# Three column counts instead of five for the matmuls of a mixture's first product

## The chip, the core and the metric

The kernel runs on one core of a Trainium2 chip. The metric is the time of one execution on the device, in microseconds (us).

## What is computed

The reference is causal attention with a decay, followed by a mixture of experts that sends every token to one expert:

```python
scores = np.where(causal, -1e9, scale * q @ k.T + decay)      # 8 batches, 8 heads, 576 tokens, 64
attn_out = softmax(scores) @ v                                # -> x: 4608 tokens x 512
expert_idx = np.argmax(x @ w_gate, axis=1)                    # 8 experts
for e in range(8):
    mask = expert_idx == e
    h = np.maximum(x[mask] @ w1[e], 0.0)                      # w1: 512 x 1024
    out[mask] = gate_w[mask, None] * (h @ w2[e])              # w2: 1024 x 512
```

How many tokens an expert gets is known only on the chip. With the inputs timed here the counts are 582, 620, 632, 571, 592, 462, 604 and 545 for experts 0 to 7.

## The kernel before

The first half of the program is attention, and nothing of it is touched. Then the experts come one after the other. Each has room for 640 tokens (`CAP`). An expert's work on TensorE (PE) is the *first product* (tokens times `w1`, line 1421, function `product`) followed by the *second product* (ReLU'd values `h` times `w2`, line 1229, function `down`). Every value is split into a rounded high part and a low rest, and a product is three matmuls: high by high, low by high, high by low.

Expert 0 has a path of its own. For experts 1 to 7 the first product is done by a scheme with seven block products in place of eight, on pairs of tokens: token columns are halved to `HN` = 320 and the tokens' and weights' blocks are combined by sums first. The work is in four rounds (`seven`, i = 0 to 3). A round has seven *steps* of 6 matmuls, in two groups: steps 0 to 3 (24 matmuls) and steps 4 to 6 (18 matmuls). The program order of every engine is pinned to the order in which the code is written. Between the groups' steps the other engines do the rest of a round:

- ACT copies the product of step 0 to `p1` (line 1475) and of step 2 to `p5` (line 1481), and makes ReLUs (`hhw`, line 1466);
- VectorE (DVE) adds `p1` (lines 1478 and 1486), combines (1487, 1494) and makes the low parts of `h` (line 1469);
- GpSimd (POOL) makes one sum, `p5` = `u3` + `p5` (line 1488), from the DVE result of line 1486, and ACT's ReLU of it comes before ACT's copy of the next round's step 0 in ACT's order;
- in the same queues stand tasks for other stages: splits of weights into high and low part (ACT lines 1333 and 1348, DVE and POOL lines 1339 and 1349), sums of the next expert's weights (POOL 1318 to 1321) and gathers of its tokens (POOL 1149).

PE's second group of a round needs `p1`, since step 4 accumulates onto the bank of step 0. The second product takes `h` in slabs of 128 rows; the fourth slab comes out of the last round, and its matmul is the tenth of the second product (the first nine are on slabs one to three, with four transposes among them for the next expert).

Since the tokens of an expert are fewer than 640, each group stands in the program several times, with 320, 304, 288, 272 and 256 columns; every copy has the same matmuls. PE reads a number from `c.arms`, made on the chip from the expert's count, and jumps to the copy that is the narrowest to hold half the count (`by_count`, line 1426, `arms`, line 1028):

```python
ARM, ARMS = 16, 5                                   # line 44
G.tensor_scalar(t, c.carry, -0.5 / ARM, HN / ARM - 0.484375, ALU.mult, ALU.add)
G.tensor_scalar(t, t, 0.0, ARMS - 1.0, ALU.max, ALU.min)
def pick(lo, hi):                                   # in by_count
    if lo == hi:
        f(HN - ARM * lo)
        return
    mid = (lo + hi + 1) // 2
    with self.tc.If(self.arm < mid) as branch:
        pick(lo, mid - 1)
    with branch.Else():
        pick(mid, hi)
```

There are 7 experts x 4 rounds x 2 groups = 56 such choices. The first matmul of steps 0 to 3 always has 320 columns, so that the whole bank is written; the other engines always work on 320 columns.

Of the kernel before, what the change touches and what calls it, by code (L numbers as in the profile page):

```python
# [40 lines left out]
CA, CB = NA * P, NB * P  # L41

HN = CAP // 2
ARM, ARMS = 16, 5
XM = 2 * (KT // 2) * HN
XN = ("T2", "T1", "T4", "T3", "B22")

# [1780 lines left out]
```

## Time and profile before

| | |
|---|---|
| median of 3 runs | 767.41 us (767.35 to 769.39) |
| the profiled execution's own time | 766.13 us |
| its span, first to last instruction | 764.4 us |
| PE busy | 741.7 us, 97% of the span |
| DVE / POOL / ACT busy | 71% / 67% / 65% |
| mean granted TensorE clock | 0.986 of full speed |
| bytes of the two queues that carry instructions | 1.49 MB and 0.36 MB |
| idle of PE just ahead of a matmul of line 1421 | 11.1 us |

The span runs from the first to the last instruction, and the time has 1.7 us more around it. A busy PE share counts matmuls from start to modelled end, and these overlap: how fast PE goes is read from the distance of matmul starts.

### The profile page before, as it was taken

To read this page: it belongs to the slowest core of one execution; us is meant where nothing else is said; L and a number is where in the kernel's file an instruction comes from. 1 tells how busy PE (TensorE), PEld (TensorE's weight loads), DVE (VectorE), ACT (ScalarE), POOL (GpSimd) and SP (SyncE) were. 2 spreads that over 40 slices of the span, in tenths; PEclk is the share of its full clock that TensorE was granted. 3 is DMA by queue.
4 is the path that set the end of the run, shared out by engine and by line. 5 is a ranking of instruction groups with operands and counts; after the bars stand their busy time and mean duration, and the time that the engine had idled before them with its cause. 6 is when DMAs were issued, how large, how long until landed. Compare 5 with 4: busy or idle time off the path is not lost.

```text
span 764.4 us, 18736 instructions
## 1 busy us (share of the span) xinstructions
PE 741.7 (97%) x6464; PEld 633.3 (83%) x6464; DVE 541.7 (71%) x1596; ACT 499.3 (65%) x1319; POOL 513.3 (67%) x681
## 2 busy tenths in 40 slices
PE   9999999999999999999989999999999889999996
PEld 5888888888888887989978888988988878978985
DVE  6668898988888887627777387486585585685720
ACT  6999998999899996525555465464554554653621
POOL 6999998989898989544864475465565465565311
PEclk8999999999999999999999999999999999999998
DMA  6957787777766674333533613622632532623200
GB/s 187 222 151 211 197 215 189 204 198 212 202 197 213 200 217 139 111 117 110 182 95 111 199 53 111 206 67 90 204 96 93 170 93 83 193 83 108 77 29 34
DMA packets 78583, 112.17 MB, mean 147 GB/s; under 512 B 9327, under 2 KB 40047, under 8 KB 78448
## 3 DMA queue, kind: packets, MB, share of 16 engines
q1 hardware_dynamic: 71408, 90.38, 41.6%
q0 software_dynamic: 6400, 19.93, 8.0%
q8 instruction: 91, 1.49, 0.8%
q14 instruction: 44, 0.36, 0.2%
q10 hardware_dynamic: 640, 0.01, 0.0%
HBM read 91.26 MB, written 20.07 MB: 146 GB/s over the span
## 4 chain that ended last, share of the span: by engine, by line
PE 85%; DVE 6%; POOL 4%; issue 2%; ACT 1%; DMA 1%; SPq 0%; POOLq 0%; DVEq 0%; ACTq 0%
PE ps L1229 29%; PE ps L1421 13%; PE ps L525 11%; PE ps L402 9%; PE ps L454 8%; PE ps L436 4%; PE ps L1195 3%; PE ps L449 3%; DVE w_1w L1349 2%; DVE hl L1469 2%; PE ps L1390 1%; PE ps L616 1%; POOL u L1488 1%; POOL w L1086 1%; ACT hhw L1466 1%
## 5 line engine op out<-in xcount | busy, mean ns | idle before, releaser
L421 ACT ACTIVATE sc<-sc,nmx 128x512 f32<-128x512 f32 (+3 forms) x256 | 142.4, 559 | 5.6 <-DVE nmx L378 4.6
L1238 POOL DMA_INDIRECT out<-y,si_fast x40 | 42.9, 1072 | 118.0 <-ACT y L1237 75.0
L1229 PE MATMUL ps<-w_0w,hhw 128*128 128x512 f32 x280 | 113.4, 405 | 2.6 <-ACT hhw L1466 2.6
L1229 PE MATMUL ps<-w_0w,hl 128*128 128x512 f32 x280 | 110.7, 395 | 0.0
L1229 PE MATMUL ps<-w_1w,hhw 128*128 128x512 f32 x280 | 110.3, 394 | 0.0
L1421 PE MATMUL ps<-X_0w,w1s 128*128 128x320 f32 (+3 forms) x504 | 107.3, 304 | 0.2 <-ACT u L1481 0.2
L466 ACT COPY aT<-ps 128x512 f32<-128x512 f32 (+1 forms) x224 | 93.3, 506 | 1.9 <-PE ps L454 1.1
L329 POOL TENSOR_TENSOR hl<-raw,hl 128x640 fp32r<-128x640 f32 (+1 forms) x60 | 89.7, 1494 | 5.0
L525 PE MATMUL ps<-aT,va_t 128*64 128x256 f32 (+3 forms) x896 | 90.3, 353 | 0.0
L1421 PEld LDWEIGHTS ps<-X_0w,w1s 128*128 128x128 f32 x504 | 83.2, 191 | 0.5 <-ACT u L1481 0.4
L1237 ACT ACTIVATE y<-ps,g_fast 128x512 f32<-128x512 f32 x40 | 27.6, 689 | 81.2 <-PE ps L1229 81.2
L402 PE MATMUL ps<-hl 64*128 64x512 f32 (+1 forms) x720 | 79.8, 339 | 0.0
L525 PEld LDWEIGHTS ps<-aT,va_t 128*64 128x64 f32 x896 | 56.1, 137 | 28.5 <-issue 5.0
L1421 PE MATMUL ps<-X_1w,w1s 128*128 128x320 f32 (+3 forms) x252 | 76.0, 301 | 0.3 <-issue 0.3
L1488 POOL TENSOR_TENSOR u<-u,u 128x320 f32<-128x320 f32 x27 | 23.8, 881 | 68.3 <-DVE u L1486 60.3
L1421 PE MATMUL ps<-xa,w1s 128*128 128x320 f32 (+3 forms) x336 | 58.4, 310 | 11.0 <-issue 3.5
L378 DVE CUSTOM_DVE_ANT_0 sc<-ps,bias 128x128 f32<-128x128 f32 (+1 forms) x128 | 59.8, 486 | 10.3 <-PE ps L402 3.7
L1229 PEld LDWEIGHTS ps<-w_0w,hhw 128*128 128x128 f32 x280 | 52.5, 187 | 14.8 <-ACT hhw L1466 4.5
L1229 PEld LDWEIGHTS ps<-w_0w,hl 128*128 128x128 f32 x280 | 52.6, 188 | 14.1 <-DVE hl L1469 1.7
L1421 PEld LDWEIGHTS ps<-xa,w1s 128*128 128x128 f32 x336 | 50.2, 193 | 15.6 <-issue 4.8
L1229 PEld LDWEIGHTS ps<-w_1w,hhw 128*128 128x128 f32 x280 | 52.7, 188 | 10.1
L378 DVE CUSTOM_DVE_ANT_1 sc<-ps,bias 128x256 f32<-128x256 f32 (+1 forms) x128 | 57.7, 487 | 3.4 <-PE ps L402 3.3
(247 smaller groups left out, 1886.7 us busy)
## 6 DMA issues: line engine op xcount, KB each, us to landing
bias<-ud SPq DMA_DIRECT2D x30, 576.0 KB, 5.9
w1r<-in_w SPq DMA_DIRECT2D x112, 128.0 KB, 2.6
w<-in_w SPq DMA_DIRECT2D x28, 512.0 KB, 5.1
raw<-in_qkT SPq DMA_DIRECT2D x64, 160.0 KB, 3.6
raw<-in_qkT SPq DMA_DIRECT2D x64, 144.0 KB, 3.6
va_t<-in_va SPq DMA_DIRECT2D x32, 256.0 KB, 5.7
x_dram<-row SPq DMA_DIRECT2D x32, 256.0 KB, 2.7
wraw<-in_w SPq DMA_DIRECT2D x7, 512.0 KB, 3.9
```

What stands on the lines that cost most here:

```text
L329: return eng.tensor_tensor(hl[:, 1], raws[n][:, r : r + w], hl[:, 0].bitcast(F32), ALU.subtract)
L378: red_last[:] = [V.tensor_tensor_reduce(dst, src, in1, -0.125, init, ALU.add, ALU.min, nms[n][:, col : col + 1]).ins]
L402: note(nc.tensor.matmul(pb[j][:, o : o + w], q[js], k[js], start=(i == 0), stop=(i == len(terms) - 1),))
L421: A.activation(x, x, AF.Exp, bias=nms[n][:, 5 * j + t : 5 * j + t + 1], scale=-1.0, accum_out=ssums[b][:, t, 2 * p + j : 2 * p + j + 1])
L436: note(nc.tensor.matmul(pb[half][:, 0:JW], q, k, start=(i == 0), stop=(i == len(terms) - 1),))
L454: note(nc.tensor.transpose(out.bitcast(F32R), words, c.identr[rows, rows]))
L466: copy_on = {"a": lambda o, i: A.copy(o, i), "v": lambda o, i: V.tensor_copy(o, i)}
L525: note(nc.tensor.matmul(pv[j * HD : (j + 1) * HD, q0 - qa : qb - qa], l, r, start=(blk == 0), stop=(blk == nb - 1),))
L1229: c.note(nc.tensor.matmul(py, rows(hi_, ft), w[wi], start=(ft + k == 0), stop=(ft == FT - 1 and k == 2),))
L1238: nc.gpsimd.indirect_dma_start(out=self.out, out_offset=bass.IndirectOffsetOnAxis(ap=si[:, s : s + 1], axis=0), in_=y, in_offset=None, bou ...
L1421: self.nc.tensor.matmul(bank[:, 0:cols], w[:, wi, mat, kt], x[xi][:, kt, 0:cols], start=start and k == 0, stop=k == 5, skip_group_check=True,)
L1488: G.tensor_tensor(p5, u3, p5, ALU.add)
```

## The change

The list of copies gets coarser: 320, 288 and 256 columns. Two of five copies of every group go, the tree of comparisons gets smaller, and a count that had taken the copy with 304 columns takes the one with 320 (272 would go to 288). Nothing else is edited.

```diff
 HN = CAP // 2
-ARM, ARMS = 16, 5
+ARM, ARMS = 32, 3
 XM = 2 * (KT // 2) * HN
```

With the counts above, experts 1 and 2 run 320 columns before and after, experts 3 and 7 run 288, expert 5 runs 256, and experts 4 and 6 go from 304 to 320.

The order of PE's instructions at the first choice, that of expert 1, round 0, steps 0 to 3 (`xa`, `X_0w`, `X_1w` are tokens' blocks, `w1s` weights' blocks, `ps` the PSUM bank):

```order
 L1441 TENSOR_LOAD arms [waits Pool_49]
 L1441 ISA x2
-L1433 COMPARE_AND_BRANCH x2
+L1433 COMPARE_AND_BRANCH
 L1421 MATMUL ps<-xa,w1s 128x320 [waits DVE_49,PE_49,Activation_49]
 L1421 MATMUL ps<-xa,w1s 128x320
```

One comparison fewer stands ahead of the widest copy; the matmuls and their waits are the same.

Behind the widest copy of the same choice, still on PE, where the copy with 304 columns stood:

```order
 L1421 MATMUL ps<-X_1w,w1s 128x320
 L1433 UNCONDITIONAL_BRANCH
-L1421 MATMUL ps<-xa,w1s 128x320 [waits DVE_49,PE_49,Activation_49]
-L1421 MATMUL ps<-xa,w1s 128x304
-L1421 MATMUL ps<-xa,w1s 128x304 [waits DVE_49]
-L1421 MATMUL ps<-xa,w1s 128x304 x3
-L1421 MATMUL ps<-X_0w,w1s 128x320 [waits PE_49,Activation_49]
-L1421 MATMUL ps<-X_0w,w1s 128x304
```

A whole copy of 24 matmuls goes there, and the one with 272 columns likewise; the jump from the end of the widest copy to the next choice then passes two copies instead of four. The other engines' instructions are the same and stand in the same order.

## Rows read from the trace of the kernel before

**Rows 1.** The page: span and instructions, busy time, the queues that carry instructions.
```profile
span 764.4 us, 18736 instructions
...
PE 741.7 (97%) x6464; PEld 633.3 (83%) x6464; DVE 541.7 (71%) x1596; ACT 499.3 (65%) x1319; POOL 513.3 (67%) x681
...
q8 instruction: 91, 1.49, 0.8%
q14 instruction: 44, 0.36, 0.2%
```

**Rows 2.** Timeline of PE: start, us, engine, line, shape, count; first matmuls of groups.
```profile
369.32 1.04 PE L1421 MATMUL ps<-xa,w1s 128*128 128x320 f32 x6
371.96 1.04 PE L1421 MATMUL ps<-xa,w1s 128*128 128x320 f32 x6
...
540.98 0.99 PE L1421 MATMUL ps<-xa,w1s 128*128 128x304 f32 x6
543.49 1.00 PE L1421 MATMUL ps<-xa,w1s 128*128 128x320 f32 x6
```

**Rows 3.** Who waited for whom, PE, us 360 to 764: us in total, times, longest.
```profile
PE ps L1421 <- issue: 3.9, 3, 2.3
PE ps L1229 <- ACT hhw L1466: 2.6, 4, 0.9
PE ps L1421 <- PE ps L1421: 2.5, 6, 0.9
PE ps L1421 <- ACT w_0w L1348: 2.3, 1, 2.3
PE ps L1421 <- ACT u L1481: 1.4, 2, 1.2
PE ps L1421 <- ACT hhw L1466: 1.0, 1, 1.0
```

**Rows 4.** Timeline of PE in expert 5, from one group into the next round.
```profile
595.48 0.87 PE L1421 MATMUL ps<-xa,w1s 128*128 128x256 f32 x6
...
600.08 1.70 PE L1421 MATMUL ps<-xa,w1s 128*128 128x320 f32 x6 [2.31 <-issue]
```

**Rows 5.** Windows behind the two longest stalls: busy of PE, PEld, DVE, ACT, POOL, granted clock, DMA.
```profile
384.80:388.10 3.30, 3.30 (x12) 3.30 (x13) 1.17 (x2) 0.45 (x1) 0.00 (x0) 0.50 0.69 225
600.10:603.20 3.10, 3.10 (x14) 3.10 (x15) 0.00 (x0) 1.38 (x3) 2.40 (x3) 0.50 0.40 81
```

**Rows 6.** Timeline of PE, ACT and DVE in expert 1, around its longest stall.
```profile
384.75 1.96 PE L1421 MATMUL ps<-xa,w1s 128*128 128x320 f32 x6 [2.28 <-ACT w_0w L1348]
...
383.17 1.05 ACT L1348 CAST w_0w<-w 128x1024 fp32r<-128x1024 f32 x1
...
387.23 0.49 DVE L1469 SCALAR_TENSOR_TENSOR hl<-ps,hhw 128x320 fp32r<-128x320 f32 x1 [1.75 <-ACT hhw L1466]
```

**Rows 7.** Timeline of DVE and PE in expert 4: line 1486, rounds 0 and 2; fourth slab.
```profile
542.91 0.48 DVE L1486 TENSOR_TENSOR u<-ps,u 128x320 f32<-128x320 f32 x1
...
556.42 0.48 DVE L1486 TENSOR_TENSOR u<-ps,u 128x320 f32<-128x320 f32 x1
...
565.04 0.50 PE L1229 MATMUL ps<-w_0w,hhw 128*128 128x512 f32 x1 [0.40 <-ACT hhw L1466]
```

**Rows 8.** The same of experts 5 (597 on), 2 (431 on) and 3 (487 on).
```profile
597.29 0.48 DVE L1486 TENSOR_TENSOR u<-ps,u 128x320 f32<-128x320 f32 x1
...
622.53 0.50 PE L1229 MATMUL ps<-w_0w,hhw 128*128 128x512 f32 x1 [0.95 <-ACT hhw L1466]
...
431.02 0.48 DVE L1486 TENSOR_TENSOR u<-ps,u 128x320 f32<-128x320 f32 x1
...
455.20 0.39 PE L1229 MATMUL ps<-w_0w,hhw 128*128 128x512 f32 x1
...
487.70 0.48 DVE L1486 TENSOR_TENSOR u<-ps,u 128x320 f32<-128x320 f32 x1
...
510.56 0.39 PE L1229 MATMUL ps<-w_0w,hhw 128*128 128x512 f32 x1
```

## The prediction

> **What bounds the kernel now.** I read the page first, then PE's timeline through the seven experts, then the list of waits, then DVE's timeline. The page has PE busy for 97% of the span, so PE's own work and PE's holes are all there is to win or lose [rows 1].
>
> PE's timeline gives the price of a column. A second group of 18 matmuls lasts from the start of its first matmul to the start of the next round's: 371.96 - 369.32 = 2.64 us at 320 columns, 146.7 ns each, and 543.49 - 540.98 = 2.51 us at 304, 139.4 ns each [rows 2]. Sixteen columns are 7.3 ns.
>
> The list of waits gives the holes. Ahead of matmuls of the first product PE is idle for 3.9 + 2.5 + 2.3 + 1.4 + 1.0 = 11.1 us, in 13 places [rows 3]. All but two of them lie at the first matmul of a group, behind a jump. For nine of them, 6.4 us, the trace names no other engine ("issue", or PE's own last matmul). One hole is plain: in expert 5 PE runs a second group of 18 in 2.0 us, then stands for 2.31 us with nothing to wait for [rows 4]. The hole that is put down to an ACT cast in expert 1 (2.28 us) is of the same kind: that cast ended at 383.17 + 1.05 = 384.22, and PE started only at 384.75, half a microsecond later [rows 6].
>
> I take these holes to be **instruction fetch**. Queue q8 moved 1.49 MB in 91 packets, 16.4 KB each [rows 1]. PE ran 6464 matmuls and 6464 weight loads; the copies that are not taken are 7 x 4 x 42 x 4 = 4704 matmuls, with loads 9408 instructions more. 1.49 MB over 12,928 + 9408 is 67 B; the 5808 instructions of the other engines (18,736 - 12,928) on q14's 0.36 MB are 62 B. Without the copies not taken, q8 would come to 115 B. So PE's code is loaded in order, copies that are jumped over included. A round is 5 x 42 x 2 = 420 instructions, 28 KB or 1.7 packets, and lasts 6.15 us at 320 columns; two jumps of such a round can ask for two packets within 2 us. In expert 5 the jump at 595.48 and the next PE start at 600.08 are 4.6 us apart [rows 4]: my estimate of how long a packet takes from the jump that asks for it until PE runs from it.
>
> [...]
>
> [...]
>
> **What else bounds: DVE's order.** Closing the holes does not give all of this back. Line 1486 on DVE feeds POOL's sum, that feeds ACT's ReLU, behind which ACT's copy of the next round stands, which lets DVE and PE go on. In expert 4 it starts at 542.91 in round 0 and at 556.42 in round 2, 6.76 us a round, though PE's round at 304 columns is 5.9. The fourth slab's matmul comes at 565.04, behind a wait for ACT: 565.04 - 542.91 = 22.13 us after the first 1486 [rows 7]. I use this as the time of the side chain wherever PE is not the slower one.
>
> **The change part by part.**
>
> *Wider matmuls, experts 4 and 6.* 2 x (168 - 16) = 304 matmuls, the openings being 320 wide already, by 7.3 ns: 2.2 us of PE. But in both experts PE waits for the fourth slab (4 such waits, 2.6 us [rows 3]), since the side chain is later. What moves the end is the start of that chain: step 5 of round 0 ends after 36 matmuls, 28 of them wider, 0.2 us. **+0.4 us** for both; 0 to +2.2 are the ends.
>
> *Fewer comparisons.* Experts 1, 2, 4, 5 and 6 save one on each of 8 choices, 40 in all. By columns alone 320 and 304 differ by 7.3 ns; at 7.3 / 16 per column a 320-wide matmul is 146 ns, so nothing is left over for the jump of a group whose next code is there [rows 2]. [...]
>
> *Less code.* Three copies make a round 252 instructions, 16.8 KB: one packet a round. A round lasts 6.15 us at 320 columns and 5.0 at 256, both above the 4.6 us a packet needs. So the holes go. What it gives, expert by expert, at the fourth slab's matmul:
>
> - Expert 1: 2.28 us of hole, 0.4 of a smaller one, and 12 matmuls at the lower clock, 1.5, are 4.2. Not all counts: DVE's idle of 1.75 us ahead of 387.23 [rows 6] goes wholly, and I count about 1 of the 1.5 us, which DVE lost later to slow matmuls; then the side chain binds. **-2.7** (0 if the cast is the cause, -4.2 if all counts).
> - Expert 2: side chain 431.02 + 22.13 = 453.15 against 455.20 [rows 8], 2.05, less 0.15 for restarting behind a wait. **-1.9** (PE alone 2.6).
> - Expert 3: 487.70 + 22.13 = 509.83 against 510.56, 0.7, less the restart. **-0.5** (what PE alone would give is in rival A).
> - Expert 5: 597.29 + 22.13 = 619.42 against 622.53 [rows 8]. **-3.1** (0 to -6).
> - Experts 4, 6 and 7: nothing. 4 and 6 wait for the side chain already; in 7 DVE is as late as PE, though POOL has no next expert there (0 to -1.5).
>
> The second products behind are PE alone and keep these gains. Sum: 0.4 - 2.7 - 1.9 - 0.5 - 3.1 = **-7.8 us**. Of the profiled execution's 766.13 us that leaves 758.3; its time is 1.3 below the median shown, so from 767.41 I forecast **759.6 us**, 1.0% faster.
>
> **The rivals.**
>
> *A: the side chain follows PE.* If DVE's order has more slack than I think, all 11.1 us of holes and both slow-clock stretches (2 x 1.5) come back, less 2.2 of widening: -11.9, **755.5 us**. For it: DVE is 71% busy. Against: 1486 kept its 6.76 us a round in expert 4 with hardly a hole [rows 7]. Chance 0.07.
>
> *B: the holes are no fetch, or the change doesn't cure it.* Late data, or a jump that costs the same over two copies as over four, would leave them; then only the widening counts, +0.4 with the side chain, +2.2 without: **767.8 to 769.6 us**, within 0.3%, which is about what a measurement of this kernel can tell (2.3 us). [...] For it: the list of waits names ACT for 4.7 of the 11.1 us [rows 3]. Against: nine holes with no releaser, and the 0.5 us after the cast [rows 6]. Chance 0.11.
>
> *C: slower by the clock.* Without holes PE arrives earlier at the fourth slab and waits for the side chain there in all seven experts, at up to 2 us each. Behind 2.28 and 2.31 us of idle the clock fell to 0.50 [rows 5]. If it fell at each, 3.2 us at half speed cost 1.6 each, 7 x 1.6 - 7.8 = +3.4, **770.8 us**. It decides against the change from five experts on. Against: by the sums above the waits are 0.5 to 2 us, all under the idle that is known to do it. Chance 0.04. In one or two experts it may well happen, which leaves -6.2 to -4.6.
>
> *D: half the holes stay*, since the 256-column round is near the packet time: about -3.5, **764 us**. Chance 0.08.
>
> **How the numbers follow.** My forecast has 0.70, with 757 to 763 as its own range (a lower clock in one or two experts, expert 1's cast, +2.2 instead of +0.4). With A at 755.5 left out and D at 764 taken in, 756.5 to 764.0 holds about 8 in 10. Faster by over 0.3% are the forecast, A and D: 0.85; same is B, 0.11; slower is C, 0.04.
>
> **What would show it.** In the changed profile: q8 at about 1.49 - 4704 x 67 B = 1.17 MB, 72 packets; the waits "issue" and "PE ps L1421" ahead of line 1421 near 0; no 0.50 clock in expert 5; second groups of experts 4 and 6 at 2.64 us; the wait of line 1229 for ACT grown from 2.6 to about 6 us, now in experts 2 and 3 too; 22.1 us from the first 1486 to the fourth slab in experts 2 to 6. I am wrong if holes without a releaser remain behind jumps, if 1486 comes faster than 6.7 us a round, or if the clock falls at the fourth slab.

## The result, and the profile after

The changed kernel takes **760.32 us** (median of four runs, 758.6 to 762.59) against 768.04 for the kernel before on the same chip: a ratio of **0.9899**, with an interval of 0.9868 to 0.993. Two more measurements gave 0.9862 (0.9806 to 0.9917) and 0.9887 (0.9845 to 0.9929). In microseconds the medians differ by 7.7, 9.9 and 8.9. The forecast was 759.6 us, 7.8 less than before. The profiled execution took 759.79 us.

The page after, the lines that answer to [rows 1]:

```profile
span 758.0 us, 18696 instructions
...
PE 739.7 (98%) x6464; PEld 631.8 (83%) x6464; DVE 541.7 (71%) x1596; ACT 499.3 (66%) x1319; POOL 515.6 (68%) x681
...
q8 instruction: 72, 1.18, 0.6%
q14 instruction: 44, 0.36, 0.2%
```

PE does as many matmuls as before; q8 went from 91 packets to 72, the number forecast, and q14, the other engines' code, stayed at 44.

The list of waits of PE from 360 us to the end, against [rows 3]:

```profile
PE ps L1229 <- ACT hhw L1466: 6.0, 7, 1.7
PE ps L1421 <- ACT u L1475: 3.0, 5, 1.0
PE ps L1421 <- ACT u L1481: 0.2, 1, 0.2
```

The two rows without a releaser ("issue" and PE's own last matmul, 6.4 us in nine places) are gone altogether, and so is the ACT cast that stood behind 2.3 us. What has come up is the side chain: at the fourth slab 6.0 us in all seven experts, and 3.0 us for `p1` (line 1475) ahead of a second group.

PE's timeline at the groups of [rows 2]:

```profile
368.72 1.04 PE L1421 MATMUL ps<-xa,w1s 128*128 128x320 f32 x6
371.36 1.04 PE L1421 MATMUL ps<-xa,w1s 128*128 128x320 f32 x6
...
537.12 1.04 PE L1421 MATMUL ps<-xa,w1s 128*128 128x320 f32 x6
539.76 1.04 PE L1421 MATMUL ps<-xa,w1s 128*128 128x320 f32 x6
```

Expert 4's second group of round 0 lasts 539.76 - 537.12 = 2.64 us, as expert 1's does; it was 2.51 at 304 columns. The side chain of expert 4, as in [rows 7]:

```profile
539.09 0.48 DVE L1486 TENSOR_TENSOR u<-ps,u 128x320 f32<-128x320 f32 x1
...
552.61 0.48 DVE L1486 TENSOR_TENSOR u<-ps,u 128x320 f32<-128x320 f32 x1
...
561.24 0.50 PE L1229 MATMUL ps<-w_0w,hhw 128*128 128x512 f32 x1 [0.43 <-ACT hhw L1466]
```

It keeps its pace: 6.76 us a round, and 561.24 - 539.09 = 22.15 us to the fourth slab, against 22.13 before. The same distance, from an expert's first matmul of line 1421 to its fourth slab's first matmul, both starts from PE's timeline, gives the table by expert (us):

| expert | before | after | change | forecast |
|---|---|---|---|---|
| 1 | 32.23 | 29.45 | -2.8 | -2.7 |
| 2 | 29.66 | 27.66 | -2.0 | -1.9 |
| 3 | 28.00 | 27.24 | -0.8 | -0.5 |
| 4 | 27.45 | 27.65 | +0.2 | +0.2 |
| 5 | 30.01 | 26.85 | -3.2 | -3.1 |
| 6 | 27.76 | 27.92 | +0.2 | +0.2 |
| 7 | 26.35 | 26.32 | 0 | 0 |

The sum is -8.4 us, while the span fell by 6.4. From the fourth slab to the next expert 1.4 us were lost in expert 1 and 1.1 us in the others together; the first expert of the table began 0.6 us earlier (365.20 against 365.81), which is the attention half and not the change. The 1.4 us lie behind the wait in expert 1. PE's timeline there, and the windows behind it and behind expert 3's wait of 1.04 us (busy of PE, PEld, DVE, ACT, POOL, granted clock, DMA):

```profile
394.65 0.58 PE L1229 MATMUL ps<-w_0w,hhw 128*128 128x512 f32 x1 [1.74 <-ACT hhw L1466]
```

```profile
394.65:398.00 3.35, 3.35 (x8) 2.48 (x9) 2.88 (x9) 2.31 (x5) 3.10 (x4) 0.54 0.00 0
...
506.10:509.40 3.30, 3.30 (x16) 2.54 (x17) 2.82 (x9) 2.58 (x7) 3.05 (x4) 1.00 0.00 0
```

After 1.74 us of idle the trace has the clock granted at 0.50 from 394.94 us on for 3.41 us, 0.54 over the window, and 8 matmuls are done where the other window has 16, four of them short transposes. The stretch from this matmul to the next expert lasts 28.9 us; in an execution of the same kernel without this fall it lasts 27.5 (below).

### The profile page after: what moved, and what is told of

Same layout as the page of the kernel before. It is cut to its first block, busy times and chain, and to the rows that moved or that the text cites. A ratio compares the mean times of both kernels' runs of the same rounds, so it can differ in the third digit from the quotient of the medians.

```text
span 758.0 us, 18696 instructions
## 1 busy us (share of the span) xinstructions
PE 739.7 (98%) x6464; PEld 631.8 (83%) x6464; DVE 541.7 (71%) x1596; ACT 499.3 (66%) x1319; POOL 515.6 (68%) x681
## 4 chain that ended last, share of the span: by engine, by line
PE 67%; DVE 15%; POOL 8%; ACT 3%; issue 3%; DMA 3%; POOLq 0%; SPq 0%; DVEq 0%; ACTq 0%
PE ps L1229 27%; PE ps L525 9%; PE ps L402 8%; PE ps L454 6%; DVE w_1w L1349 5%; PE ps L1421 4%; DVE hl L1469 3%; PE ps L436 3%; PE ps L1195 2%; POOL u L1488 2%; PE ps L449 2%; ACT hhw L1466 2%; DVE w1s L1339 2%; POOL w L1086 1%; DVE u L1486 1%
## 5 line engine op out<-in xcount | busy, mean ns | idle before, releaser
L1421 PE MATMUL ps<-X_0w,w1s 128*128 128x320 f32 (+2 forms) x504 | 107.4, 303 | 0.2 <-ACT u L1481 0.2
L1237 ACT ACTIVATE y<-ps,g_fast 128x512 f32<-128x512 f32 x40 | 27.6, 690 | 82.4 <-PE ps L1229 76.8
L1421 PE MATMUL ps<-X_1w,w1s 128*128 128x320 f32 (+2 forms) x252 | 75.7, 301 | 0.0
L1421 PE MATMUL ps<-xa,w1s 128*128 128x320 f32 (+2 forms) x336 | 56.2, 302 | 3.0 <-ACT u L1475 3.0
L1339 DVE TENSOR_TENSOR w1s<-w1r,w1s 128x1024 fp32r<-128x1024 f32 (+1 forms) x42 | 49.1, 1183 | 12.0 <-ACT w1s L1333 10.2
```

Of the source, the lines that this page charges most:

```text
L1339: (eng or self.nc.vector).tensor_tensor(lo, raw, hi.bitcast(F32), ALU.subtract)
L1421: self.nc.tensor.matmul(bank[:, 0:cols], w[:, wi, mat, kt], x[xi][:, kt, 0:cols], start=start and k == 0, stop=k == 5, skip_group_check=True,)
```

## The experiments

**The code, or the columns?** Five copies as before, but with the columns that the changed kernel gives each expert:

```diff
 # of the kernel before, ARM, ARMS = 16, 5
-                f(HN - ARM * lo)
+                f(HN - 2 * ARM * ((lo + 0) // 2))
```

> Five copies as before, but the second is 320 and the fourth 288 columns wide, so that every expert runs the columns of the changed kernel with the code volume of the old one. Fetch theory: the holes ahead of first groups stay (about 11 us of idle, q8 at 1.49 MB), and only the widening is added, +0.4 us: 768.4 us, ratio 1.000 to 1.001. If PE paid for the columns in full: +2.2, 770.2 us. Rival (the choice of columns, not the code, made the gain): 760.3 us.

769.14 us, ratio **0.9997** (0.9966 to 1.0029): the gain is gone with the code. q8 is back at 91 packets, and so are the holes:

```profile
PE ps L1421 <- issue: 7.1, 7, 2.5
PE ps L1421 <- ACT w_0w L1348: 3.8, 2, 2.3
PE ps L1421 <- PE ps L1421: 2.1, 3, 1.0
...
PE ps L1421 <- ACT hhw L1466: 0.5, 1, 0.5
```

They are 13.5 us here against 11.1, and some sit in other places: expert 6 has its fourth slab at 29.9 us instead of 27.8. In expert 5 the hole of [rows 4] stands where it stood, between the same two groups:

```profile
598.20 0.87 PE L1421 MATMUL ps<-xa,w1s 128*128 128x256 f32 x6
...
602.94 1.12 PE L1421 MATMUL ps<-xa,w1s 128*128 128x320 f32 x6 [2.46 <-issue]
```

602.94 - 598.20 = 4.7 us from one jump to PE's start behind the next; it was 4.6.

**The same columns with less code.** Four copies, 320, 304, 288 and 256: every expert runs the columns of the kernel before, and what goes is the copy that none takes.

```diff
 # of the kernel before, ARM, ARMS = 16, 5
-            if lo == hi:
+            if lo == hi or (lo, hi) == (2, 3):
 ...
-            mid = (lo + hi + 1) // 2
+            mid = 4 if (lo, hi) == (2, 4) else (lo + hi + 1) // 2
```

> 320, 304, 288 and 256 columns: every expert runs exactly the columns of the kernel before, and only the copy that no expert takes (272) is gone. Fetch theory: a round is 336 instructions, 1.3 packets, so 6.1 us at 320 columns give one packet in 4.6 us, the time that I estimated a packet needs: most holes go in experts with 320 and 304 columns, and some stay in experts 3, 5 and 7; q8 at 1.33 MB, 81 packets; 760 to 764 us. If the gain were in the number of comparisons (8 fewer here, against 40): 0.2 of the gain, 766.5 us. If the gain needed the wider copies: 768 us.

762.72 us (757.59 to 763.22, eight runs), ratio **0.9917** (0.9888 to 0.9945), with 81 packets. Taking away one copy that is never run is worth more than half of the change: 0.8% of its 1.0 to 1.4%. The holes without a releaser shrink to one, in expert 4, which still starts late behind a jump:

```profile
PE ps L1229 <- ACT hhw L1466: 6.7, 7, 1.7
PE ps L1421 <- ACT u L1475: 2.1, 5, 0.6
PE ps L1421 <- ACT hhw L1466: 1.4, 1, 1.4
PE ps L1421 <- issue: 0.5, 1, 0.5
```

The 1.4 us that the list puts down to an ACT ReLU, in expert 5, is probably another: PE starts at 601.77 us, 1.8 us after a packet of q8 has landed, which is how the holes of the kernel before end too (below). The profiled execution was the fastest of the eight, 757.59, so its rows show the good end. Of the five that lie near 763 it is known only that their mean granted clock was 0.989 or 0.990, against 0.992 to 0.996 in the other three.

**Comparisons.** The changed kernel with two more comparisons, always true, ahead of the copies of 320 and 288 columns, 96 in all that are run:

```diff
 # of the changed kernel
-                f(HN - ARM * lo)
+                with ExitStack() as st:
+                    for _ in range(2 if lo < ARMS - 1 else 0):
+                        st.enter_context(self.tc.If(self.arm < lo + 1))
+                    f(HN - ARM * lo)
```

> The changed kernel with two comparisons more, always true, ahead of each group in the copies of 320 and 288 columns: 96 more are run, and each choice has some 8 instructions more. Hidden-branch theory: matmuls already queued cover them, 0 to +0.3 us: 760.5 us, and the distance of matmul starts across a group's edge stays at 146 ns. [...]

759.85 us (757.79 to 762.78), ratio 0.9894 (0.9832 to 0.9956): between the changed kernel's 0.9862 and 0.9899. It is 1.6 us above the changed kernel's median on the same chip (758.26), by estimate 17 ns for each of the 96, inside the intervals. PE's starts across the edge of a group are those of the changed kernel, 2.64 us for 18 matmuls:

```profile
536.85 1.04 PE L1421 MATMUL ps<-xa,w1s 128*128 128x320 f32 x6
539.49 1.04 PE L1421 MATMUL ps<-xa,w1s 128*128 128x320 f32 x6
```

Expert 3's fourth slab came 1.1 us late in this execution; DVE waited there 0.97 us for an ACT cast of weights (line 1333), not for PE. PE's list of waits has one new row, 1.1 us in expert 1 put down to a DVE cast (line 1349); whether that is a wait for data or a fetch of the longer code was not settled.

**No choice at all.** Every group once, 320 columns:

```diff
 # of the changed kernel
-        pick(0, ARMS - 1)
+        f(HN)
```

> No choice at all: each group stands once, 320 columns for every expert. Side-chain theory: in experts 3, 5 and 7 the first 1486 comes 0.3, 0.7 and 0.3 us later and the side chain moves with it; expert 7 becomes bound by PE (24.6 + 2.4 us from its first matmul to the fourth slab, against 26.3 now). Together about +1.9 us to the changed kernel, 760 to 763 us; q8 at 54 packets, 0.88 MB. Rival (PE pays for every column): 32 columns more in experts 3 and 7, 64 in expert 5, 152 matmuls each, 0.46 ns a column: +8.9 us, 769 us.

761.62 us (758.8 to 765.87), ratio 0.99 (0.9848 to 0.9951), with 52 packets. Experts 3, 5 and 7 reach the fourth slab at 27.6, 27.6 and 26.7 us after their first matmul, 0.35, 0.73 and 0.35 later than with choices: +1.4 us (1.9 was expected), where the columns alone would be 8.9. PE's waits fall to 3.9 us at the slab and 0.2 for `p1`: the narrow copies mostly bought waiting time. The profiled execution lost the clock twice, near the start (0.50 from 9 to 12 us) and in expert 1 (0.68 over 3.2 us), and with 765.87 us is the longest of the four.

**The side chain.** The changed kernel with POOL's gather of the next expert's first tokens moved behind round 3:

```diff
-                       (20, N(self.sums_s, 0)), (20, fetch(e + 1, 0)),
+                       (20, N(self.sums_s, 0)), (27, fetch(e + 1, 0)),
```

> The changed kernel with one POOL gather (the next expert's first tokens) moved from behind step 6 of round 2 to behind step 6 of round 3, so that POOL's line 1488 of round 3 no longer stands behind it. Side-chain theory: 1488 starts 0.7 to 0.8 us earlier, the fourth slab 0.6 us in experts 2, 4 and 6 (PE is then the later one) and 0.75 in experts 3 and 5, expert 1 unchanged since DVE is late there: -3.3 us, 756 to 758 us. Rival (the waits for ACT at the fourth slab have another cause, or the gather is then late for the transposes): no gain, 760 us.

757.66 us (756.44 to 759.33), ratio **0.9855** (0.9806 to 0.9904). The fourth slab comes at 27.05, 26.43, 27.04, 26.08 and 27.12 us in experts 2 to 6, sooner by 0.6, 0.8, 0.6, 0.8 and 0.8: 3.6 us, where 3.3 was expected. But over the whole of these experts only 0.9 to 1.5 us of it is left, against three profiled executions of the changed kernel, and the median lies only 0.6 us below two of that kernel's three (2.7 below the first), inside the intervals: the expected gain of 3.3 us in time did not come. A new wait stands right behind the slab:

```profile
PE ps L1421 <- ACT u L1475: 3.0, 5, 1.0
PE ps L1229 <- ACT hhw L1466: 2.8, 4, 1.7
PE ps L1229 <- DVE hl L1469: 2.0, 6, 0.4
```

The third matmul of the slab reads its low part, and DVE is late with that. DVE and POOL in expert 2 of this kernel, and DVE's same instruction in the changed kernel:

```profile
451.11 1.02 DVE L1469 SCALAR_TENSOR_TENSOR hl<-u,hhw 128x320 fp32r<-128x320 f32 x1
...
450.69 0.97 POOL L1149 DMA_INDIRECT xg<-x_dram,gi_fast  x1
```

```profile
450.88 0.49 DVE L1469 SCALAR_TENSOR_TENSOR hl<-u,hhw 128x320 fp32r<-128x320 f32 x1 [0.84 <-ACT hhw L1466]
```

Beside the gather the same DVE instruction takes 1.02 us instead of 0.49. It ends 0.47 us behind the gather's end (452.13 against 451.66), and 0.45 to 0.47 us behind it in experts 1 and 3 to 6 as well: as if it ran only once the gather was over.

**The clock in expert 1.** Seven matmuls of 512 columns at the head of expert 1's second product, into the bank that the first real one overwrites:

```diff
+        if (e, m, part[0]) == (1, 0, 0):
+            for _ in range(7):
+                nc.tensor.matmul(py, rows(0, 0), self.w2p[e, 0][0], start=True, stop=True)
```

> The changed kernel with seven matmuls more (512 columns, overwritten) at the head of expert 1's second product: 1.6 us of work in front of a wait of 1.7 us. Clock theory: PE's idle there falls to about 0.1 us, the fourth slab comes at the same time after the expert's first matmul (29.4 us), the clock behind it is 1.00 in every look. Against executions in which it fell, 1.4 us less; against the others, nothing: a median 0 to 1 us below the changed kernel's. Rival (PE's work sets the end there): +1.6 us.

758.80 us (757.78 to 761.83), ratio 0.9887. The filler costs nothing: the fourth slab comes 29.44 us after expert 1's first matmul, within 0.01 us what it was, with some 0.1 us of idle ahead of it, and the expert lasts 56.9 us from first matmul to first matmul where the changed kernel's profiled execution had 58.4. Two more profiled executions of the changed kernel show that this is not a fixed price. Of the first repeat, the window behind the same wait, here 1.72 us:

> The changed kernel once more, as the measure for the others of this set: 760.3 us (758.6 to 762.6 so far), ratio about 0.990 to before. Expert 1 is the place to watch: if the 1.74 us wait ahead of its fourth slab is what lowered the clock there, the clock share of its second product should again be 0.94, and a run in which it stays at 1.00 should be about 1.4 us shorter.

```profile
397.33:400.60 3.27, 3.27 (x16) 2.54 (x17) 2.80 (x9) 2.56 (x7) 3.11 (x4) 1.00 0.00 1
```

Of the second repeat, the window behind a wait of 1.73 us:

> The changed kernel in more rounds, to stand beside the next one on the same chip: 758 to 760.5 us, ratio 0.988 to 0.990. Whether the clock falls behind the 1.7 us wait in expert 1 is open: it did in one of three looks so far.

```profile
396.29:399.60 3.31, 3.31 (x9) 2.44 (x10) 2.84 (x9) 2.31 (x5) 3.08 (x4) 0.60 0.01 2
```

The first kept the clock, the second lost it. They took 758.26 and 758.25 us as medians, with profiled lengths of expert 1 of 57.0 and 58.1 us. The execution that kept the clock was not shorter as a whole, as had been expected: 759.99 us against 759.79, since its expert 1 began 2.7 us later. Behind the same wait the clock stayed at 1.00 with four copies and with the later gather, too, and was 0.68 in the version without choices: it fell in three of six. Behind the filler, here and in the two runs of both edits, it stayed at 1.00 in three of three, too few to show that the filler keeps it. Where the clock would have fallen the filler could save 1.4 us, elsewhere nothing; its median is not clear of the changed kernel's.

**Both edits.** The later gather and the filler together, measured twice:

> Both of the last two edits: if they are independent, -3.3 us and up to -1 us against the changed kernel, 755 to 758 us.

> The later gather and the filler once more, in more rounds. By the times of the fourth slab it would be 3.3 us below the changed kernel; by the lengths of the whole experts, where matmuls on the low part of the fourth slab now wait for DVE (2.1 us), about 1 us, and up to 1.4 more in executions in which the clock falls in expert 1: 756.5 to 758.5 us, ratio 0.985 to 0.987.

757.02 us, ratio 0.9858 (0.9806 to 0.9911), then 757.08 us, 0.9879 (0.9838 to 0.9921), beside 758.25 and 0.9887 for the changed kernel; the second ratio is just outside what was expected. It is the version with the lowest medians and clearly beats the kernel before; that it beats the changed kernel, by about 1 us, lies inside the intervals and is not shown.

## Why the prediction was right

*The holes are instruction fetch, and they go with the code.* Shown. With the columns fixed and the code put back, the gain is gone (0.9997); with the old columns and one unused copy less, more than half of it is there (0.9917). The trace also has q8's packets themselves, and they tell what the list of waits could not: each of the 13 holes of the kernel before ends 1.4 to 2.0 us after a packet of q8 has landed, those put down to ACT included (packet 597.42 to 598.36, PE at 600.08; packet 382.12 to 383.04, PE at 384.75). So do the 13 of the five copies with new columns, while of the groups that start without a hole about a fifth start so. One hole of the kernel before, 1.0 us in expert 5 that is put down to a ReLU, ends 0.1 us behind that ReLU and may be a wait for it as well. The packets a round agree: with five copies, 420 instructions or 1.7 packets of 16.4 KB a round, PE has holes at jumps, and with three, 252 instructions or one packet, it has none without a releaser. Rival B, by which the holes stay, is out.

*The time of a fetch was mis-sized.* The forecast took 4.6 us as what a packet needs, and judged by it that a round of one packet is safe. In the hole of [rows 4] from which the 4.6 us were read, the packet took 0.94 us, and PE started 2.66 us after the packet had (2.3 to 3.1 in the 13); 1.9 of the 4.6 us passed before it began. Packets of the kernel before started as little as 3.05 us apart. That the holes go was right, but how near a round may come to the limit no run shows.

*Comparisons are free here, as far as the intervals tell.* 96 more of them left the starts as they were, 2.64 us for 18 matmuls, and moved the time by no more than the changed kernel's own medians differ (759.85 us beside 758.25 to 760.32). For the 40 that the change saves that leaves nothing, as forecast.

*The columns cost only what the side chain lets through.* +0.2 us in experts 4 and 6, as forecast, though PE's work grew by 2.2. (Of the 36 matmuls up to step 5, 32 are wider and not 28; the 0.2 us stays.) The version without choices shows it on a larger scale: 1.4 us at the fourth slabs for 8.9 us of columns.

*The side chain takes over where the holes leave off.* The forecast's constant of 22.13 us held to 0.02 in expert 4 and to 0.3 in experts 2 to 6 (22.09 to 22.43), and the seven terms came out within 0.3 us each. (The 1.5 us for slow matmuls, in expert 1's term and in rival A, are [rows 5] less [rows 2]: 3.30 us for 12 matmuls at the clock of 0.50 less 12 x 0.147.) The moved gather confirms one of its links: POOL's sum of round 3 starts 0.8 us sooner in experts 2 to 6 without that gather ahead of it. Rival A, by which the side chain follows PE and 11.9 us come back, is out: line 1486 kept its 6.76 us a round.

*What the forecast did not carry into its sum* is the stretch behind the fourth slab. Apart from 0.15 us for a restart in experts 2 and 3 it took the second products as unchanged, and they were not: 1.4 us more in expert 1 behind the fall of the clock, in the profiled execution, and 1.1 us in the others. Half of these 1.1 are in expert 3, whose second product lasts 27.55 us from the fourth slab to the next expert and lasted 27.03. Of that, 0.25 us is the restart: the first three matmuls behind the new wait take 0.94 us, and took 0.69 without one. The rest comes of starts 233 ns apart instead of 229 through the remaining matmuls, with no wait among them. Both distances occur in both kernels, and the second repeat of the changed kernel has 27.22 us behind the same wait; what sets them is open.

That -7.8 met the measured -7.7 so closely is in part luck: the first product gave -8.4, the stretch behind took 2.5 and the earlier start gave 0.6, so that the two profiled spans differ by 6.4, while the three pairs of medians differ by 7.7 to 9.9. Rival C's mechanism did occur, in the one expert with the longest wait, and a fall of the clock at the fourth slab was among the forecast's own signs of being wrong. The argument against C, that waits under the known idle of 2.28 us are safe, did not hold, since the clock fell behind 1.74 us in some executions.

## What to carry to other kernels

Code that is never run had a price here where control flow jumps over it: one copy that no expert takes, 10 of 91 packets, made 0.8%. Before adding a narrower copy of a loop body, compare the packets of code from one jump to the next, and the time between the jumps, with how fast packets come in the trace (here 16.4 KB at least 3.05 us apart, and PE running 2.3 to 3.1 us after a packet's start). Look for holes at the first instruction behind a jump that have no releaser, or one whose end lies well before, and see whether a packet of the instruction queue landed shortly ahead of the hole's end. And price a gain at the instruction where the next engine is already late, not on the engine whose holes close: 11 us of holes and 3 us of slow clock were worth 8 to 10.

## What had not been expected of the hardware

- The clock's answer to an idle of 1.72 to 1.74 us differs between executions of the same kernel: 0.54 and 0.60 behind it in two, 1.00 in a third. Behind the 1.04 us of expert 3 it stayed at 1.00.
- The same happens near the start. The attention half is the same code in every version, and expert 1's first matmul came between 364.7 and 369.9 us. From 9 to 12 us the clock was granted at 0.50 in the first repeat of the changed kernel and at 1.00 with four copies:

```profile
9.00:12.00 3.00, 3.00 (x12) 1.45 (x12) 1.31 (x4) 0.48 (x1) 2.71 (x8) 0.50 0.82 241
```

```profile
9.00:12.00 3.00, 3.00 (x22) 2.05 (x18) 2.16 (x8) 2.25 (x8) 2.46 (x8) 1.00 0.81 228
```

  How much of the spread of 1 to 7 us among a kernel's runs this fall makes was not tried.
- A DVE instruction with both operands in SBUF (`hl<-u,hhw`, line 1469) took twice its time (1.02 against 0.49 us) beside a POOL gather, and ended 0.45 to 0.47 us behind the gather in six experts. It isn't the gather alone: in expert 7 of the changed kernel, which has no gather, the same instruction takes 0.90 and 0.87 us beside POOL's long sum of weights (line 1339), and 0.48 with POOL idle.
